# Loading the first x chunk and the first w1 tiles of an MLP in two pieces each, with fewer dummy matmuls before layer 1

## The chip, the cores and the metric

The kernel runs on one core of a Trainium2 chip. The metric is the device time of one execution in microseconds (us). Each call for runs also times the kernel before on the same chip. The profile of a run is of one execution; its span is about 1.3 us shorter than the time of that execution (93.4 against 94.75).

Each run carries a state. On one core a run is called slow when it is over 1.5% above the fastest run of the same kernel. That label comes from the time alone.

## The reference

```
B, S, D, F = 1, 2048, 448, 1792        # bf16
h   = gelu(x @ w1 + b1)                # layer 1: D = 3*128 + 64 in the contraction
out = h @ w2 + b2                      # layer 2
```

## The kernel before

All engines are programmed by hand with semaphores. x is worked on in four chunks of 512 rows. Chunks 1 to 3 are transposed by the DMA. The first chunk is loaded plainly into `xn`, turned on TensorE (12 transposes of 128x128, and two more for the 64 remainder columns), and copied from PSUM to `xT`. Until x is there, TensorE runs dummy matmuls on constants.

```python
NWARM = 7
W1CUTS = (0, 4, 8, 14)                        # w1's tiles of 128 columns per transfer

pr.dma("sync", lambda e: e.dma_start(xn[:, :, :], x0v), "x")      # whole first chunk, 448 KB
pr.barrier("sync", ["table"])                 # the rest waits for the activation table
load_w1r(0); load_w1(1); load_w1r(1); load_w1(2); ...             # SyncE's queue
load_w1(0, "scalar")                          # w1's first four tiles, 384 KB, ScalarE's queue
# ... cut ...
warm(NWARM)          # 7 dummies of 512 columns
warm(1, HC)          # one of 256
turn_all()           # 12 + 2 transposes, copies to xT on VectorE and ScalarE
warm(1, HC)          # one of 256
turn_b1()            # VectorE: bias to its layout
# VectorE: copy of half of w1's remainder rows to the other partitions, in two pieces
for i in (0, 1):
    ...  pr.op("vector", ... tensor_copy(odd(slice(0, H)), odd(slice(H, P))), after=[("w1r", i)], ...)
L = [Layer1(0, j) for j in range(NPAIR)]
for h in (0, HC):            # 24 matmuls of 256 columns, in pairs on 64 rows each (64*128 in the trace)
    L[0].a(h, h + HC)
    L[1].a(h, h + HC)
L[0].b()                     # 6 of 512 columns, then the pair on the remainder rows
L[2].a()
# ... cut: the rest of layer 1, layer 2, the other chunks: one unbroken stream of matmuls
```

Of the kernel before, what the change touches and what calls it, by code (L numbers as in the profile page):

```python
# [73 lines left out]
def bass_standalone__dense_activation_gelu__prompt_kernel(  # L74
# [8 lines left out]
    B, S, D = x.shape  # L83
# [4 lines left out]
    HC = SC // 2  # L88
# [4 lines left out]
    KT = 3  # L93
    D3 = KT * P
    DH = D // 2
    NWARM = 7

    with ExitStack() as es:
        sb = lambda name, shape, dt: es.enter_context(nc.sbuf_tensor(name, shape, dt))
        xn = sb("xn", [P, STC, D], BF16)  # L100
        xr = sb("xr", [P, STC // 2, P], BF16)
        ident = sb("ident", [P, P], BF16)
# [14 lines left out]
        pr = Program(nc, es)  # L117
# [2 lines left out]
        ones_m = one.broadcast_to([P, SC])  # L120


        W1CUTS = (0, 4, 8, 14)

        def w1_of(ft):
            return max(i for i, c in enumerate(W1CUTS) if c <= ft)

        def load_w1(i, engine="sync"):
            c0, c1 = W1CUTS[i] * P, W1CUTS[i + 1] * P
            pr.dma(engine, lambda e: e.dma_start(  # L130
                w1_sb[:, :, c0:c1], w1[0:D3, c0:c1].rearrange("(k p) f -> p k f", p=P)), ("w1", i))
# [3 lines left out]
        def load_w1r(i, engine="sync"):  # L135
            cs = slice(RCUTS[i] * P, RCUTS[i + 1] * P)
            pr.dma(engine, lambda e: e.dma_start(w1r[H:P, cs], w1[D3:D, cs]), ("w1r", i))

        def load_w2(a, b):
            pr.dma("sync", lambda e: e.dma_start(  # L140
                w2_sb[:, a:b, :], w2[a * P:b * P, :].rearrange("(f p) d -> p f d", p=P)), ("w2", a))
# [8 lines left out]

        x0v = x2[0:SC, :].rearrange("(p t) d -> p t d", t=STC)
        o0v = out2[0:SC, :].rearrange("(p t) d -> p t d", t=STC)
        pr.dma("sync", lambda e: e.dma_start(xn[:, :, :], x0v), "x")
        pr.barrier("sync", ["table"])
        load_w1r(0)
        load_w1(1)
        load_w1r(1)
        load_w1(2)
        load_w2(0, 7)
        load_w2(7, 14)  # L160
        pr.dma("sync", lambda e: e.dma_start(b2_bc[:, :], b2.partition_broadcast(P)), "b2")
        for c in range(1, NSC):
            for slot in range(KT + 1):
# [10 lines left out]
               after=["b1z"])  # L174
        pr.op("scalar", lambda e: e.activation(junk[:, :], one, ACT.Gelu_apprx_tanh), event="table")  # L175
        load_w1(0, "scalar")

        def turn_b1():
            for q in range(4):
                pr.op("vector", lambda e, q=q: e.transpose(  # L180
                    b1t[32 * q:32 * q + 32, :], b1n[:, 32 * q:32 * q + 32]), after=["b1n"], event=("b1t", q))
            pr.op("vector", lambda e: e.tensor_copy(b1_f[:, :], b1t[:, 0:NFT]),
                  after=[("b1t", q) for q in range(4)], event="b1")
# [5 lines left out]
        def warm(n, cols=SC):  # L189
            for _ in range(n):  # L190
                pr.op("tensor", lambda e: e.matmul(unit[0][:, 0, 0:cols], lhsT=ones_w, rhs=ones_m[:, 0:cols],  # L191
                                                   start=True, stop=True))
# [140 lines left out]
        def stage(t):  # L333
            return unit[3 - t // 2][:, t % 2, 0:2 * P].bitcast(BF16)

        def turn(t):
            for k in range(KT):
                pr.op("tensor", lambda e, k=k: e.transpose(  # L338
                    stage(t)[:, k * P:(k + 1) * P], xn[:, t, k * P:(k + 1) * P], ident[:, :]),
                    after=["ident", "x"], event=("xt", t) if k == KT - 1 else None)  # L340

        def evac(engine, t):
            o = xT[:, 0:KT, t * P:(t + 1) * P]
            i = stage(t)[:, 0:D3].rearrange("p (k s) -> p k s", k=KT)
            pr.op(engine, lambda e: e.copy(o, i) if engine == "scalar" else e.tensor_copy(o, i),  # L345
                  after=[("xt", t)], event=("xT0", t))
            busy[(3 - t // 2, t % 2)] = ("xT0", t)

        def turn_all():


            pr.op("vector", lambda e: e.tensor_copy(  # L352
                xr[:, :, :].rearrange("p q (two h) -> p q two h", two=2),
                xn[:, :, D3:D].rearrange("p (q two) h -> p q two h", two=2)), after=["x"], event="xr_in")
            for t in range(STC):
                turn(t)
                evac(("vector", "scalar")[t % 2], t)
            for q in range(STC // 2):
                pr.op("tensor", lambda e, q=q: e.transpose(  # L359
                    stage(0)[:, q * P:(q + 1) * P], xr[:, q, :], ident[:, :]),  # L360
                    after=["xr_in", ("xT0", 0)], event=("xr", q))
            halves = (slice(0, H), slice(H, P))
            for src, engine in enumerate(("vector", "scalar")):
                i = stage(0)[halves[src], 0:2 * P].rearrange("p (q s) -> p q s", q=2)
                for dst in (src, 1 - src):
                    o = xT[halves[dst], KT, 0:SC].rearrange("p (q two s) -> p q two s", q=2, two=2)[:, :, src, :]
                    pr.op(engine, lambda e, o=o, i=i, engine=engine:
                          e.copy(o, i) if engine == "scalar" else e.tensor_copy(o, i),  # L368
                          after=[("xr", 0), ("xr", 1)], event=("xR0", dst, src))
            busy[(3, 0)] = ("xR0", 1, 0)  # L370
            busy[(3, 2)] = ("xR0", 0, 1)

        warm(NWARM)
        warm(1, HC)
        turn_all()
        warm(1, HC)
        turn_b1()

        for i in (0, 1):
# [3 lines left out]
                  after=[("w1r", i)], event=("w1rU", i))  # L383
# [12 lines left out]
        for c in range(NSC):  # L396
# [7 lines left out]
            else:  # L404

                pr.op("vector", lambda e: e.tensor_copy(b2_z[H:H + 1, :], b2_bc[H:H + 1, :]),  # L406
                      after=["b2", "b2z0"], event="b2z")
# [3 lines left out]
            p = Layer2(c, (0, 1))  # L411
            if c + 1 < NSC:
                q = Layer2(c, (2, 3))
# [5 lines left out]
            else:  # L419
                q, r = Layer2(c, (2,)), Layer2(c, (3,), True)  # L420
# [37 lines left out]
```

## Time and profile before

Three runs gave 94.43 us (94.25 to 94.45), and the profiled execution took 94.75 us.

| what | value | where to read it |
|---|---|---|
| PE on the chain that ended last | 97% of 93.4 us | chain of waits |
| unbroken matmuls of the two layers | 5.86 to 91.27 us | chain of waits |
| x: issued, landed | 0.75, about 3.86 us | timeline and transfers (3.1 us to landing) |
| start of layer 1 | 5.79 us | timeline |
| layer 1's first 30 matmuls | 2.52 us | timeline |

The chain of work that ended last, in order of time; columns are start, length and what.

```profile
0.78 3.36 PE u L191 x8
4.14 1.29 PE u L338 x12
5.43 0.21 PE u L359 x2
5.65 0.21 PE u L191
5.86 85.41 PE u L216 x909
91.27 0.38 DVE out_sb L325
```

TensorE is the only engine on it until the last 0.38 us. The change can only act before 5.86 us. The timeline of PE at the start; columns are start, length, engine, line and operation, and `xN` counts merged instructions (L191 are dummies, L338 and L359 transposes, L216 the layers).

```profile
0.78 3.36 PE L191 MATMUL u<-const-bfloat16-1.0 128*128 128x512 bf16 x8 [0.78 <-PEq L443]
4.00 1.44 PE L338 MATMUL u<-ident,xn 128*128 128x128 bf16 x12
5.23 0.42 PE L359 MATMUL u<-ident,xr 128*128 128x128 bf16 x2
5.44 0.42 PE L191 MATMUL u<-const-bfloat16-1.0 128*128 128x256 bf16 x1
5.79 2.52 PE L216 MATMUL u<-xT,w_sb 64*128 64x256 bf16 x30
8.15 0.38 PE L216 MATMUL u<-xT,w1r 64*128 64x512 bf16 x2
```

The table of stretches shows why; the number behind PE's busy time counts the matmuls that touch the stretch, and the 1.00 before the DMA share is the granted clock.

```profile
5.80:6.60 0.80, 0.80 (x9) 0.58 (x10) 0.73 (x3) 0.75 (x3) 0.00 (x0) 1.00 0.89 255
6.60:7.40 0.80, 0.80 (x19) 0.69 (x14) 0.61 (x3) 0.14 (x1) 0.00 (x0) 1.00 0.88 234
```

Both stretches are fully busy with the same kind of matmul, yet the second holds twice as many. Single starts in the trace agree: pairs of 256 columns start 213 ns apart up to 6.6 us and 109 ns apart after. (The prediction's 208 and 107 count from the second start of a pair to the first of the next.) TensorE's rate doubled near 6.6 us. The column of the granted clock says 1.00 in both and does not show this: the packed trace of this execution holds no record of the clock (0 entries), and the view then prints 1.00.

### The profile page before, as it was taken

The numbers are of one execution on the slowest core, as the hardware profiler recorded it, in microseconds if no ns is written. First come the engines' busy times: TensorE is split into PE (matmuls) and PEld (weight loads), VectorE is DVE, ScalarE is ACT, GpSimd is POOL, SyncE is SP. The second block draws the span as 40 slices with busy tenths as digits, with TensorE's granted clock in tenths as the row PEclk, the third lists the DMA queues.
The fourth block names the chain that finished last, engine by engine and source line by source line (L and its number), as shares of the span: only waits on it lengthen the run. The fifth ranks groups of instructions, "written<-read, shape, count | busy, mean of one in ns | idle before, by whom it ended". The sixth has DMA issues, their size and how long they took to land.

```text
span 93.4 us, 2060 instructions
## 1 busy us (share of the span) xinstructions
PE 90.4 (97%) x932; PEld 46.5 (50%) x932; DVE 13.3 (14%) x33; ACT 38.5 (41%) x63; POOL 1.7 (2%) x8
## 2 busy tenths in 40 slices
PE   6999999999999999999999999999999999999990
PEld 2475444455544444454554444445544444475890
DVE  0173001010334000000234000000234000000421
ACT  6073787900002887900002888900001878910001
POOL 6000000000000000000000000000000000000000
DMA  2999999554748000000033000000022000000022
GB/s 51 358 275 292 360 309 151 113 113 91 83 86 217 7 0 0 7 0 0 0 102 101 0 0 4 0 7 0 0 98 98 0 0 7 0 0 7 18 80 98
DMA packets 12344, 7.32 MB, mean 78 GB/s; under 512 B 6960, under 2 KB 12144, under 8 KB 12336
## 3 DMA queue, kind: packets, MB, share of 16 engines
q1 hardware_dynamic: 11904, 6.80, 31.1%
q10 hardware_dynamic: 400, 0.39, 1.2%
q8 instruction: 7, 0.11, 0.5%
q14 instruction: 1, 0.01, 0.0%
q0 software_dynamic: 32, 0.00, 0.0%
HBM read 3.79 MB, written 1.84 MB: 60 GB/s over the span
## 4 chain that ended last, share of the span: by engine, by line
PE 97%; DVE 0%; issue 0%
PE u L216 91%; PE u L191 4%; PE u L338 1%; DVE out_sb L325 0%; PE u L359 0%
## 5 line engine op out<-in xcount | busy, mean ns | idle before, releaser
L268 ACT ACTIVATE g<-u,b_f 128x512 bf16<-128x512 f32 x56 | 35.0, 685 | 40.3 <-PE u L216 40.3
L216 PE MATMUL u<-w_sb,g 64*128 64x448 bf16 (+1 forms) x504 | 43.2, 328 | 0.0
L216 PE MATMUL u<-xT,w_sb 64*128 64x512 bf16 (+1 forms) x348 | 41.2, 372 | 0.0
L216 PEld LDWEIGHTS u<-w_sb,g 64*128 64x128 bf16 x504 | 24.4, 94 | 18.6
L216 PEld LDWEIGHTS u<-xT,w_sb 64*128 64x128 bf16 x348 | 16.9, 95 | 19.6 <-issue 0.3
L311 DVE TENSOR_TENSOR out_sb<-u,b_bc 128x448 bf16<-128x448 f32 x14 | 8.1, 619 | 60.6 <-PE u L216 60.6
L216 PE MATMUL u<-xT,w1r 64*128 64x512 bf16 x56 | 10.6, 376 | 0.0
L191 PE MATMUL u<-const-bfloat16-1.0 128*128 128x512 bf16 (+1 forms) x9 | 3.8, 578 | 0.8 <-PEq L443 0.8
L216 PEld LDWEIGHTS u<-xT,w1r 64*128 64x128 bf16 x56 | 2.7, 94 | 3.3
L328 ACT CAST out_sb<-u 128x224 bf16<-128x224 f32 x1 | 0.3, 346 | 9.2 <-PE u L216 9.2
L191 PEld LDWEIGHTS u<-const-bfloat16-1.0 128*128 128x128 bf16 x9 | 1.2, 138 | 2.4 <-issue 2.4
L345 ACT COPY xT<-u 128x384 bf16<-128x384 bf16 x2 | 1.0, 479 | 2.8 <-PE u L338 2.8
L175 ACT ACT_TABLE_LOAD x1 | 1.3, 1283 | 0.7 <-PEq L443 0.7
L338 PEld LDWEIGHTS u<-ident,xn 128*128 128x128 bf16 x12 | 1.2, 140 | 0.5 <-issue 0.5
L338 PE MATMUL u<-ident,xn 128*128 128x128 bf16 x12 | 1.4, 307 | 0.0
L186 DVE COPY xT<-xT 64x512 bf16<-64x512 bf16 x3 | 0.9, 290 | 3.5 <-DMA xT<-in_x_dram 3.5
L406 DVE COPY b_z<-b_bc 1x448 bf16<-1x448 bf16 x1 | 0.3, 267 | 6.8 <-DMA b_bc<-in_b_dram 6.8
L319 DVE TENSOR_TENSOR out_sb<-u,b_bc 128x448 bf16<-128x448 f32 x1 | 0.6, 625 | 1.7 <-PE u L216 1.7
L180 DVE STREAM_TRANSPOSE b1t<-b1n 32x32 bf16<-32x32 bf16 x4 | 0.8, 202 | 0.1
L345 DVE COPY xT<-u 128x384 bf16<-128x384 bf16 x2 | 0.7, 357 | 0.7 <-PE u L338 0.7
L368 ACT COPY xT<-u 64x256 bf16<-64x256 bf16 x2 | 0.7, 368 | 0.0
L352 DVE COPY xr<-xn 128x256 bf16<-128x256 bf16 x1 | 0.2, 227 | 3.0 <-DMA xn<-in_x_dram 3.0
(18 smaller groups left out, 5.0 us busy)
## 6 DMA issues: line engine op xcount, KB each, us to landing
out_dram<-out_sb SPq DMA_DIRECT2D x16, 112.0 KB, 1.7
w_sb<-in_w_dram SPq DMA_DIRECT2D x2, 784.0 KB, 8.7
w_sb<-in_w_dram SPq DMA_DIRECT2D x1, 576.0 KB, 6.4
xn<-in_x_dram SPq DMA_DIRECT2D x1, 448.0 KB, 3.1
w_sb<-in_w_dram ACTq DMA_DIRECT2D x1, 384.0 KB, 4.2
w_sb<-in_w_dram SPq DMA_DIRECT2D x1, 384.0 KB, 4.1
xT<-in_x_dram SPq DMA_TRANSPOSE x12, 4.5
w1r<-in_w_dram SPq DMA_DIRECT2D x1, 160.0 KB, 4.0
```

Of the source, the lines that this page charges most:

```text
L175: pr.op("scalar", lambda e: e.activation(junk[:, :], one, ACT.Gelu_apprx_tanh), event="table")
L180: pr.op("vector", lambda e, q=q: e.transpose(b1t[32 * q:32 * q + 32, :], b1n[:, 32 * q:32 * q + 32]), after=["b1n"], event=("b1t", q))
L186: pr.op("vector", lambda e: e.tensor_copy(xT[0:H, KT, s0:s1], xT[H:P, KT, s0:s1]), after=after, event=event)
L191: pr.op("tensor", lambda e: e.matmul(unit[0][:, 0, 0:cols], lhsT=ones_w, rhs=ones_m[:, 0:cols], start=True, stop=True))
L216: o = pr.op("tensor", lambda e: e.matmul(unit[u][:, lo, cols], lhsT=lhsT, rhs=rhs, start=start, stop=stop, skip_group_check=skip), after=a ...
L268: pr.op("scalar", lambda e, lo=lo, ft=ft: e.activation(g[:, ft, c * SC:(c + 1) * SC], unit[u][:, lo, :], ACT.Gelu_apprx_tanh, bias=b1_f[:, ...
L311: pr.op("vector", lambda e, lo=lo, j=j: e.tensor_tensor(out=out_sb[:, j, :], in0=unit[u][:, lo, 0:D], in1=b2_bc[:, :], op=ALU.add), after= ...
L319: pr.op("vector", lambda e: e.tensor_tensor(out=out_sb[:, j, :].rearrange("p (two h) -> p two h", two=2), in0=unit[u][:, :, 0:DH], in1=b2_ ...
L328: pr.op("scalar", lambda e: e.copy(out_sb[:, j, DH:D], unit[u][:, 1, 0:DH]), after=[y[1]], event=("o", j, 1))
L338: pr.op("tensor", lambda e, k=k: e.transpose(stage(t)[:, k * P:(k + 1) * P], xn[:, t, k * P:(k + 1) * P], ident[:, :]), after=["ident", "x ...
L345: pr.op(engine, lambda e: e.copy(o, i) if engine == "scalar" else e.tensor_copy(o, i), after=[("xt", t)], event=("xT0", t))
L368: e.copy(o, i) if engine == "scalar" else e.tensor_copy(o, i),
```

## The change

The intent is to start the transposes when the first half of x has landed, to let w1's first tiles arrive in smaller pieces, and to drop the dummies that an earlier x makes needless.

```diff
-    NWARM = 7
+    NWARM = 6
-        W1CUTS = (0, 4, 8, 14)
+        W1CUTS = (0, 2, 4, 8, 14)
-        pr.dma("sync", lambda e: e.dma_start(xn[:, :, :], x0v), "x")
+        for h in (0, 2):
+            pr.dma("sync", lambda e, h=h: e.dma_start(xn[:, h:h + 2, :], x0v[:, h:h + 2, :]), ("x", h))
         load_w1(0, "scalar")
+        load_w1(1, "scalar")
-                    after=["ident", "x"], ...)
+                    after=["ident", ("x", t // 2 * 2)], ...)
         warm(NWARM)
-        warm(1, HC)
         turn_all()
-        warm(1, HC)
         turn_b1()
# (cut: later w1 pieces renumbered; the remainder's copy on VectorE made per half of x)
```

More of the change, by code (lines that the diff above doesn't have):

```diff
@@ L152, in bass_standalone__dense_activation_gelu__prompt_kernel @@
         o0v = out2[0:SC, :].rearrange("(p t) d -> p t d", t=STC)
-        pr.dma("sync", lambda e: e.dma_start(xn[:, :, :], x0v), "x")
+        for h in (0, 2):
+            pr.dma("sync", lambda e, h=h: e.dma_start(xn[:, h:h + 2, :], x0v[:, h:h + 2, :]), ("x", h))
         pr.barrier("sync", ["table"])
         load_w1r(0)
-        load_w1(1)
+        load_w1(2)
         load_w1r(1)
-        load_w1(2)
+        load_w1(3)
         load_w2(0, 7)
@@ L339, in turn @@
                     stage(t)[:, k * P:(k + 1) * P], xn[:, t, k * P:(k + 1) * P], ident[:, :]),
-                    after=["ident", "x"], event=("xt", t) if k == KT - 1 else None)
+                    after=["ident", ("x", t // 2 * 2)], event=("xt", t) if k == KT - 1 else None)
         def evac(engine, t):
@@ L349, in turn_all @@
         def turn_all():
-            pr.op("vector", lambda e: e.tensor_copy(
-                xr[:, :, :].rearrange("p q (two h) -> p q two h", two=2),
-                xn[:, :, D3:D].rearrange("p (q two) h -> p q two h", two=2)), after=["x"], event="xr_in")
             for t in range(STC):
+                if t % 2 == 0:
+                    pr.op("vector", lambda e, t=t: e.tensor_copy(
+                        xr[:, t // 2, :].rearrange("p (two h) -> p two h", two=2), xn[:, t:t + 2, D3:D]),
+                        after=[("x", t)], event=("xr_in", t // 2))
                 turn(t)
@@ L360, in turn_all @@
                     stage(0)[:, q * P:(q + 1) * P], xr[:, q, :], ident[:, :]),
-                    after=["xr_in", ("xT0", 0)], event=("xr", q))
+                    after=[("xr_in", q), ("xT0", 0)], event=("xr", q))
             halves = (slice(0, H), slice(H, P))
```

## The prediction

> **What bounds it.** TensorE. The chain of waits puts 97% of the 93.4 us span on PE, 91% on the layer matmuls, in one unbroken piece from 5.86 to 91.27 us. The change touches only what comes before. In the timeline: dummies from 0.78 us, 12 transposes from 4.00, two for the remainder from 5.23, one dummy at 5.44, layer 1 from 5.79. The x transfer (issued 0.75) lands 3.1 us after its issue, about 3.86, so PE is fed by dummies just until x is there.
>
> **Clock.** The start-to-start times of single matmuls show two rates: dummies of 512 columns every 427 ns and transposes every 107 ns up to 5.44, and the first layer-1 pairs of 256 columns every 208 ns; from about 6.63 us the same pairs come every 107 ns. So about 0.84 us of layer 1 runs at half rate. [...]
>
> **What changes.** Removed from the PE queue: one full dummy (427 ns), the 256-column one before the transposes (213 ns) and the one after them (213 ns, plus about 0.14 us until layer 1 starts). Added: one transfer issue on each queue (0.39 and 0.45 us, off PE) and one small VectorE copy (the whole copy took 0.23 us). The bytes are the same; w1's pieces fall from 1024 to 512 bytes.
>
> **Order of transfers.** Before, w1's first packet came at 3.08 us, when x's were nearly done, although both were issued within 0.05 us. So I expect first half of x, first half of w1, second half of x, second half of w1; [...] Packets of x ran 1.77 to 3.37 us, those of w1 3.08 to 4.51, and landing is seen about 0.5 us after the last packet. My estimate: first half of x lands near 3.3, w1's first half 4.0, x's second half 4.5, w1's second half 5.2.
>
> **PE after.** Dummies end at 3.30, six transposes 3.35 to 4.0, PE idle about 0.5 us, six more 4.6 to 5.25, two remainder transposes to 5.46, layer 1 from about 5.6 instead of 5.79. So the second half of x, later than before, takes back most of the gain from the first. VectorE's chain (bias turn, remainder copy) still fits.
>
> **Worth.** 0.2 us earlier at the half rate is only 0.1 us if the rate still doubles near 6.6 us: about 94.3 us. The danger is the clock: [...] I give that one chance in three. If instead the halves of x land one behind the other (3.3 and 3.9), layer 1 starts near 5.0 and the gain is 0.4 us.
>
> **Prediction.** 94.3 us, range 93.6 to 96.1; faster by over 2%: 0.02, within 2%: 0.89, slower by over 2%: 0.09.
>
> **Right or wrong shows in:** the landing of the two halves of x (transfers view); an idle of PE of about 0.5 us between sixth and seventh transpose, put down to x; the start of layer 1 near 5.6; the moment when pairs of 256 columns fall from about 208 to 107 ns; an unchanged steady part from there to the end.
>
> **What would make it wrong:** [...] the second half of x landing before w1's first; 512-byte pieces so slow that w1's second half or the next w1 transfer stalls layer 1.

The sum came to 94.3 us: the 94.4 of before less 0.1 for a start 0.2 us earlier at the half rate. A term for a later doubling brought the sum to 96.0 us and was given one chance in three.

## The result, and the profile after

The changed kernel took 95.88 us (95.71 to 96.14, 4 runs) against 94.44 us; the ratio is 1.0152 (1.0118 to 1.0187). A ratio is the mean time of one kernel's fast runs over that of the other's in the same rounds, so it is not quite the ratio of the medians. By the 2% rule it counts as the same, but 1.4 us were lost.

The chain of waits after:

```profile
1.20 3.65 DMA xn<-in_x_dram
4.84 0.05 issue
4.89 0.82 PE u L340 x6
5.71 0.21 PE u L362 x2
5.93 86.30 PE u L218 x909
92.22 0.38 DVE out_sb L327
```

The second half of x is now on the chain and lands at 4.84 us. Still, the layers begin only 0.07 us later than before (5.93 against 5.86). The last matmul, however, is 0.95 us later (92.22 against 91.27). The timeline of PE, and the stretches:

```profile
0.78 2.72 PE L193 MATMUL u<-const-bfloat16-1.0 128*128 128x512 bf16 x6 [0.78 <-PEq L444]
3.68 0.80 PE L340 MATMUL u<-ident,xn 128*128 128x128 bf16 x6 [0.18 <-DMA xn<-in_x_dram]
4.89 0.82 PE L340 MATMUL u<-ident,xn 128*128 128x128 bf16 x6 [0.41 <-DMA xn<-in_x_dram]
5.50 0.42 PE L362 MATMUL u<-ident,xr 128*128 128x128 bf16 x2
5.86 3.42 PE L218 MATMUL u<-xT,w_sb 64*128 64x256 bf16 x30
9.11 0.38 PE L218 MATMUL u<-xT,w1r 64*128 64x512 bf16 x2
```

```profile
5.80:6.60 0.80, 0.80 (x10) 0.57 (x10) 0.53 (x2) 0.78 (x2) 0.00 (x0) 1.00 1.16 361
6.60:7.40 0.80, 0.80 (x12) 0.56 (x10) 0.68 (x5) 0.39 (x2) 0.00 (x0) 1.00 1.03 189
```

The 30 matmuls take 3.42 us instead of 2.52 and wait for nothing. In 6.60 to 7.40 there are 12 instead of 19: the rate is still low, and by the starts in the trace it doubles only near 8.5 us. So 0.90 us (3.42 less 2.52) and the 0.07 us of the later start make, to 0.01 us, the 0.96 us by which the spans differ (94.40 and 93.44). Nothing else in the kernel is slower: from the remainder pair on (8.15 and 9.11 us) to the last matmul both need the same time to 0.01 us. The other 0.5 us of the measured 1.44 has no trace: the profiled run was the slowest of the kernel before and the fastest of the changed one.

The ends of the two holes: by the semaphores in the trace the first half of x landed at 3.54, w1's first half at 4.15, x's second half at 4.84, w1's second half at 5.58 us. The single dummies stream for 427 ns each, so TensorE had nothing to do from 3.29 to 3.68 and from 4.27 to 4.89 us, 1.0 us together. (The profile's own idle of 0.18 and 0.41 is shorter because it lists a matmul for longer: the last dummy, started at 2.87, for 0.63 us.)

### The profile page after: what moved, and what is told of

Read it like the earlier page. It is cut to its first block, busy times and chain, and to the rows that moved or that the text cites. A ratio compares the mean times of both kernels' runs of the same rounds, so it can differ in the third digit from the quotient of the medians.

```text
span 94.4 us, 2057 instructions
## 1 busy us (share of the span) xinstructions
PE 90.8 (96%) x929; PEld 46.6 (49%) x929; DVE 13.6 (14%) x34; ACT 38.6 (41%) x63; POOL 1.7 (2%) x8
## 4 chain that ended last, share of the span: by engine, by line
PE 93%; DMA 4%; SPq 0%; DVE 0%; issue 0%
PE u L218 91%; DMA xn<-in_x_dram 4%; PE u L340 1%; SPq L154 0%; DVE out_sb L327 0%; PE u L362 0%
## 5 line engine op out<-in xcount | busy, mean ns | idle before, releaser
L218 PE MATMUL u<-xT,w_sb 64*128 64x512 bf16 (+1 forms) x348 | 42.1, 379 | 0.0
L218 PEld LDWEIGHTS u<-xT,w_sb 64*128 64x128 bf16 x348 | 17.4, 98 | 19.9 <-issue 0.2
L193 PE MATMUL u<-const-bfloat16-1.0 128*128 128x512 bf16 x6 | 2.7, 626 | 0.8 <-PEq L444 0.8
L193 PEld LDWEIGHTS u<-const-bfloat16-1.0 128*128 128x128 bf16 x6 | 0.7, 136 | 1.9 <-issue 1.9
```

The lines of the kernel that those rows point to most:

```text
L193: pr.op("tensor", lambda e: e.matmul(unit[0][:, 0, 0:cols], lhsT=ones_w, rhs=ones_m[:, 0:cols], start=True, stop=True))
L218: o = pr.op("tensor", lambda e: e.matmul(unit[u][:, lo, cols], lhsT=lhsT, rhs=rhs, start=start, stop=stop, skip_group_check=skip), after=a ...
```

## The experiments

Theories, by the names that the expectations use:

- A: idle of TensorE before layer 1 delays the doubling of its rate.
- B: the later half of x and the smaller pieces cost the time themselves.
- C: transposes do not count as activity; the amount of matmul work does.
- D: the moment of doubling falls by chance, alike in every kernel.
- E, formed on the way: both. Chance moves the moment of doubling from one execution to the next, and the kernel's holes let it come late in some or all of them.

The twelve runs were made in three calls, on three chips. The result above came from an earlier call; it is called the result's call.

### First call: holes filled, dummies alone, transfers alone

`fill_holes`: the changed kernel with its holes filled.

```diff
-    NWARM = 6
+    NWARM = 7
             for t in range(STC):
+                if t == 2:
+                    warm(2, HC)
                 turn(t)
```

> The changed kernel (transfers split, no dummy before layer 1) with dummies put into its two holes: a seventh full one at the start and two of 256 columns between the third and the fourth chunk-half (before the seventh transpose). Theory A (idle of TensorE before layer 1 delays the doubling of its clock): doubling back near 6.6 us instead of 8.6, layer 1 still from about 5.86, time 94.3 to 94.7 us. Theory B (the later second half of x and the smaller pieces cost the time themselves): 95.7 to 96.1, as the changed kernel. Theory C (transposes do not count as activity, only the amount of matmul work does): doubling earlier than in the changed kernel by about the 0.85 us of added dummies, 95.3 or so.

Measured: 94.65 us (94.48 to 94.76, 4 runs), before 94.21 (93.95 to 94.77, 7 runs), ratio 1.0032 (0.9987 to 1.0077). Layer 1 starts no earlier than in the changed kernel, and the transfers are the same, but the 30 matmuls take 2.13 us:

```profile
5.89 2.13 PE L218 MATMUL u<-xT,w_sb 64*128 64x256 bf16 x30
```

The changed kernel was not run in this call, so the two times alone can't be set against each other. The trace can: with the same transfers and as late a layer 1, its span is 93.4 us, as in the kernel before, so theory B is out as the explanation of the 1.4 us. The doubling came at 5.9 us, earlier than in the first trace of the kernel before, which A did not foresee.

`few_dummies`: the transfers of before, the dummies of the change.

```diff
-    NWARM = 7
+    NWARM = 6
         warm(NWARM)
-        warm(1, HC)
         turn_all()
-        warm(1, HC)
```

> The kernel before, transfers untouched, with only the dummies of the change: six full ones, none of 256 columns. One hole of about 0.65 us before the transposes, layer 1 from about 5.58 us. Theory A: the clock doubles later than 6.63 us (up to 8.6), time 95 to 96 us. Theory B: transfers are as before, so 94.3 us or a little less than before. Theory C: 1.07 us less... 0.85 us of dummies less, doubling 0.6 us or more later, about 94.7.

Measured: 94.36 us (93.88 to 94.52, 4 runs), ratio 0.9995 (0.9943 to 1.0047).

```profile
0.78 2.72 PE L191 MATMUL u<-const-bfloat16-1.0 128*128 128x512 bf16 x6 [0.78 <-PEq L441]
4.11 1.44 PE L338 MATMUL u<-ident,xn 128*128 128x128 bf16 x12 [0.60 <-DMA xn<-in_x_dram]
5.69 2.13 PE L216 MATMUL u<-xT,w_sb 64*128 64x256 bf16 x30
```

This is a miss for A in its simple form: 0.8 us without work (3.30 to 4.11), and the rate was still doubled when layer 1 began. It is also a miss for C: only six dummies came before, less matmul work than in any kernel above, and the doubling was early.

`split_only`: the transfers of the change, with all dummies of before (`NWARM = 7` and both of 256 columns).

> Only the transfers of the change: x and w1 in two pieces each, all dummies of the kernel before kept (seven, one of 256, one of 256 after the transposes). PE idle about 0.25 us before the seventh transpose, layer 1 from about 6.06 us. Theory A: doubling near 6.6 to 6.8 us, time 94.5 to 94.8 us. Theory B: 95.7 or more. Theory C: 94.5.

Measured: 94.56 us (94.28 to 94.71, 4 runs), ratio 1.0018 (0.9962 to 1.0074). The new transfers alone cost nothing that the runs resolve, though layer 1 starts at 5.88 us. They also gain nothing.

`long_dummies`: the kernel before with `NWARM = 20`, to watch the doubling under plain matmuls.

> The kernel before with 20 full dummies instead of 7, so that nothing but back-to-back matmuls runs for the first 6 us and more. Not meant to be fast: it shows when the clock doubles without transposes and without a hole. If [...] transposes count as activity: dummies go from 427 to 214 ns apart near 6.6 us, as in the kernel before. If transposes do not count (theory C): near 4 to 5 us.

Measured: 96.92 us (one run, state unknown; longer for the extra dummies). The dummies start 427 ns apart up to 4.15 us and about 219 apart from 4.52 on, so the rate doubled near 4.5 us. The transposes, now after the doubling, start 56 ns apart instead of 107. In the groups of the kernel before (L338, 311 ns) and of this one, the three numbers are the least, the median and the greatest duration in ns:

```profile
L338 PE MATMUL u<-ident,xn x12: 264/311/311, 4.0 to 5.1; 128*128 128x128 bf16 x12
```
```profile
L338 PE MATMUL u<-ident,xn x12: 217/219/220, 7.0 to 7.7; 128*128 128x128 bf16 x12
```

So transposes run at the doubled rate as other matmuls do. (They are the kernel's `transpose` calls; the trace lists them as MATMUL.) And in the same call the moment of doubling (4.5, and 5.6 to 5.9 in the three others) was not that of the first trace (6.6).

### Second call: the changed kernel again, one hole at a time, another order

`after_again`: the changed kernel, unchanged.

> The changed kernel once more, on the chip of this call, because the earlier experiments and the first result came from different calls and the moment of doubling moved between them (6.63 us in the first trace of the kernel before; about 5.6 us with few_dummies, split_only and fill_holes). Theory A [...]: 95.4 to 96.1 us here too, doubling after 7.5 us. Theory D (the moment of doubling falls by chance, whatever the kernel, and the changed kernel had bad luck in its first call): like few_dummies, 94.3 us, doubling near 5.6 us.

Measured: 94.43, 94.35, 94.40, 94.29, 95.89 and 94.51 us; before 94.55 (94.08 to 94.83, 11 runs). The ratio of 0.9983 (0.9956 to 1.001) hides that there are two groups. The profiled run was an early one:

```profile
3.85 0.67 PE L340 MATMUL u<-ident,xn 128*128 128x128 bf16 x6 [0.35 <-DMA xn<-in_x_dram]
5.04 0.51 PE L340 MATMUL u<-ident,xn 128*128 128x128 bf16 x6 [0.52 <-DMA xn<-in_x_dram]
5.59 2.13 PE L218 MATMUL u<-xT,w_sb 64*128 64x256 bf16 x30
7.57 0.74 PE L218 MATMUL u<-xT,w1r 64*128 64x512 bf16 x2
```

It is the same program as in the first profile after, with the same two holes, and its rate doubled at 4.3 us, among the transposes (a gap of 74 ns after gaps of 107), instead of 8.5. So the kernel alone does not fix the moment. Theory A alone is out. The last line shows a second thing: the remainder pair now waits about 0.14 us, because the copy on VectorE that it needs was timed for a later layer 1 (the next start comes after 359 ns instead of 216). This takes back part of the gain of an early doubling.

`fill_first` (the changed kernel with `NWARM = 7`) and `fill_second` (the changed kernel with the two dummies before the seventh transpose, `NWARM = 6`):

> The changed kernel with seven dummies instead of six: its first hole of 0.39 us closed, the second (now 0.5 us) left. Theory A: the total idle before layer 1 falls from 1.0 to 0.55 us, less than in few_dummies (0.8), which doubled early: so 94.4 to 94.8 us. Theory D: the same as after_again.

> The changed kernel with two dummies of 256 columns before the seventh transpose: its second hole of 0.62 us nearly closed (0.2 left), the first of 0.39 us left. Theory A, by the sum of idle alone: 94.4 to 94.8 us, as fill_first. If it is one hole's place that matters, the two runs differ by about 1 us. Theory D: the same as after_again.

Measured: 94.52 us (94.34 to 94.70, 6 runs) and 94.42 us (94.34 to 94.66, 6 runs), ratios 0.9995 (0.9969 to 1.0021) and 0.9987 (0.9959 to 1.0015). In their traces the doubling came near 6.3 and 6.0 us:

```profile
5.89 2.29 PE L218 MATMUL u<-xT,w_sb 64*128 64x256 bf16 x30
5.83 2.21 PE L218 MATMUL u<-xT,w_sb 64*128 64x256 bf16 x30
```

None of the twelve runs was late. That does not yet show that one hole alone is harmless: in this call only one of six runs of the changed kernel, with both holes, was late, and none of twelve is no surprise beside that.

`x_first`: to bring x's second half ahead of w1, everything on SyncE's queue.

```diff
+        load_w1(0)
+        load_w1(1)
         pr.barrier("sync", ["table"])
-        load_w1(0, "scalar")
-        load_w1(1, "scalar")
-    NWARM = 6
+    NWARM = 7
```

> A version that may beat both: the two halves of x and then the two pieces of w1, all on SyncE's queue, seven dummies. x's second half should land near 4.0 us instead of 4.84, since no piece of w1 goes before it, w1's second piece near 5.5 as in the changed kernel; no hole before the transposes; layer 1 from about 5.25 us. If the clock has doubled by then, 93.9 us; if it doubles near 6.6, 94.2. A stall of 0.2 to 0.4 us at the remainder step of the first pair of tiles is likely (the copy on VectorE is late).

Measured: 94.85 us (94.69 to 95.35, 6 runs), ratio 1.0037 (1.0007 to 1.0067). The two halves of x landed at 3.39 and 3.91 us, as hoped, and the rate doubled at 4.7 us in the middle of the transposes. But w1's pieces landed at 5.45 and 6.08 us and its next transfer at 8.90, and layer 1 had to wait for them:

```profile
5.49 2.43 PE L218 MATMUL u<-xT,w_sb 64*128 64x256 bf16 x30 [0.37 <-DMA w_sb<-in_w_dram]
8.95 0.60 PE L218 MATMUL u<-xT,w_sb 64*128 64x512 bf16 x4 [0.81 <-DMA w_sb<-in_w_dram]
```

Putting these pieces on one queue only moved the wait from x to w1.

### Third call: the two groups, a hole alone, two attempts at a better kernel

`after_third`: the changed kernel once more.

> The changed kernel a third time. So far 4 of 4 timed runs near 95.9 us in the first call and 1 of 6 in the second; the other five near 94.4. Theory E [...]: two groups again, near 94.4 and near 95.9 us and little between, in a share that chance decides. Theory D (chance alone, every kernel alike): then the kernel before should show runs near 95.9 too, which it has not in 22 runs.

Measured: 95.94, 96.03, 94.31, 95.64, 96.00 and 95.83 us, with a granted clock of 1.0 in the profiled one; before 94.01 (93.81 to 94.81, 11 runs). Because one run is at 94.31, the four above 95.7 are labelled slow here. The ratio of 1.008 (0.9998 to 1.0163) is of one run from each group and means nothing. The profiled run, of the late group, doubled near 8.65 us:

```profile
6.11 3.36 PE L218 MATMUL u<-xT,w_sb 64*128 64x256 bf16 x30
```

The size of the holes does not part the two groups: by the starts they add up to 1.01 us in the first trace after and 1.26 us here, both late, and to 1.24 us in `after_again`, which was early.

Over the result's call and the two here the changed kernel had 10 of 16 runs at 95.64 to 96.14 us and 6 at 94.29 to 94.51, none between. The kernel before had 33 runs over all four calls, none above 94.83; in the three calls that had both kernels it was 26 runs, none late, against 10 of 16. Kernels with the changed transfers and at least one hole filled (`fill_holes`, `fill_first`, `fill_second`, `split_only`) had 20 runs, none above 94.76, but 8 of them in a call without the changed kernel and 12 in the call where it was late once. Theory D is out.

`four_dummies`: the kernel before with a hole and nothing else.

```diff
-    NWARM = 7
+    NWARM = 4
         warm(NWARM)
-        warm(1, HC)
         turn_all()
-        warm(1, HC)
```

> The kernel before, transfers untouched, with four full dummies and no other: TensorE works from 0.78 to 2.44 us, then sits idle about 1.6 us until x is there (few_dummies, with six, sat idle 0.8 us and was as fast as the kernel before). Theory E: [...] 94.9 to 96.5 us, none near 94. Theory B (transfers) and D (chance): as few_dummies, 93.9 to 94.5 us.

Measured: 95.77, 95.20, 94.92, 95.44, 96.11 and 95.35 us, ratio 1.0132 (1.0086 to 1.0178). Layer 1 starts earlier than before, at 5.58 us, and the 30 matmuls take 3.76 us:

```profile
0.79 1.86 PE L191 MATMUL u<-const-bfloat16-1.0 128*128 128x512 bf16 x4 [0.79 <-PEq L441]
4.00 1.44 PE L338 MATMUL u<-ident,xn 128*128 128x128 bf16 x12 [1.35 <-DMA xn<-in_x_dram]
5.58 3.76 PE L216 MATMUL u<-xT,w_sb 64*128 64x256 bf16 x30
```

No transfer was touched. Taking dummies away, which only makes idle, is enough to lose 1.3%. Theory E said every run late, between 94.9 and 96.5 us, none near 94; that is what came (94.92 to 96.11), while the kernel before had 11 runs in this call, none above 94.81.

`copy_early`: the kernel before, with VectorE's first remainder copy ahead of the turning of b1.

```diff
-        turn_b1()
         for i in (0, 1):
+            if i:
+                turn_b1()
             odd = ...
```

> The kernel before with one VectorE step moved: the copy of w1's remainder rows that layer 1 needs first goes ahead of the turning of b1. Where the clock doubles early, layer 1 was seen to stall 0.14 us for it (few_dummies; 355 against 216 ns between two pairs). Expected gain up to 0.15 us in runs that double early, nothing in the others: ratio 0.998 to 1.000.

Measured: 94.24 us (93.96 to 94.83, 6 runs), ratio 1.0012 (0.9968 to 1.0057). Inconclusive: no gain is seen. Its trace doubled near 6.7 us, where the copy is in time anyhow.

`x_then_w1`: x in halves, w1's four tiles in one transfer on ScalarE's queue, held back until the activation table is loaded.

```diff
-        load_w1(0, "scalar")
+        load_w1(0, "scalar", ["table"])
# and x in two halves, NWARM = 7, no dummies of 256 columns, the copy early
```

> A version that may beat both: x in two halves on SyncE's queue; w1's first four tiles in one transfer on ScalarE's queue, but issued only after the activation table (about 2.2 us), so that it doesn't get between the halves of x; seven dummies, no hole; copy of the remainder rows early as in copy_early. First half of x should land near 3.5, second near 4.0, w1 near 5.0 to 5.2; layer 1 from about 5.35 us instead of 5.69 to 5.79. 93.9 to 94.2 us, no run near 95.9. If w1 comes later than 5.4, no gain.

Measured: 95.05, 95.18, 95.22, 96.94, 96.61 and 95.59 us, ratio of the fast runs 1.011 (1.0065 to 1.0156). The two highest are labelled slow, 96.94 with a granted clock of 0.982; what made them so is not known. A miss. x landed at 3.39 and 3.91 us and the transposes were done early, but w1, issued at 2.27 us in the company of SyncE's next transfers, landed at 6.45 instead of about 5, and TensorE waited:

```profile
6.49 2.13 PE L217 MATMUL u<-xT,w_sb 64*128 64x256 bf16 x30 [1.07 <-DMA w_sb<-in_w_dram]
```

No version beat the kernel before.

### All traces against theory E

Eight of the 14 packed traces hold a record of the clock. It begins with a stretch at full clock, and where the starts of matmuls resolve the doubling, this stretch begins within about 0.02 us of it.

For each trace I take the moment of doubling from this record (marked *) or, where there is none, read it from the starts, which draw together. (In `x_then_w1` TensorE was idle at that moment; only the record shows it.) Beside it stand the start and length of layer 1's first 30 matmuls, from the timeline of PE.

| kernel | rate doubles near, us | the 30 matmuls start, us | they take, us |
|---|---|---|---|
| changed, second call | 4.25* | 5.59 | 2.13 |
| long_dummies | 4.46* | 8.23 | 2.13 |
| x_first | 4.7 | 5.49 | 2.43, with waits for w1 |
| few_dummies | 5.64* | 5.69 | 2.13 |
| split_only | 5.64* | 5.88 | 2.13 |
| fill_holes | 5.90* | 5.89 | 2.13 |
| fill_second | 6.03* | 5.83 | 2.21 |
| x_then_w1 | 6.07* | 6.49 | 2.13 |
| fill_first | 6.3 | 5.89 | 2.29 |
| before | 6.6 | 5.79 | 2.52 |
| copy_early | 6.7 | 5.89 | 2.50 |
| changed, result's call | 8.55 | 5.86 | 3.42 |
| changed, third call | 8.65 | 6.11 | 3.36 |
| four_dummies | 8.94* | 5.58 | 3.76 |

No trace lies between 6.7 and 8.55 us. The three late ones are of the two kernels with 1.0 us or more of idle before the last transpose: 1.01 and 1.26 us in the changed kernel, about 1.6 in `four_dummies` (from 2.44 us, when its dummies have streamed, to the first transpose at 4.00). But the changed kernel with 1.24 us also gave the earliest doubling of all. `few_dummies`, with 0.8 us, doubled at 5.64, and none of its 4 runs was late. That is what E says in outline: chance moves the moment, and enough idle lets it come late. How much idle is enough, over what time it counts, and what chance acts on, the traces do not show.

## Why the prediction was right or wrong

The 95.88 us lie in the range of 93.6 to 96.1, and the clock, through which the loss came, was named as the danger. The central figure of 94.3 was not met. The range holds both groups of runs, so it would have held the result whichever came; that the late one came was a draw, as the second call shows (five of six runs at 94.29 to 94.51 us).

- The order of transfers was right: x, w1, x, w1. The times were put too early: 3.3, 4.0, 4.5 and 5.2 us expected, 3.54, 4.15, 4.84 and 5.58 measured.
- Hence the hole of "about 0.5 us" was two holes of 0.39 and 0.62 us. The start of layer 1 "from about 5.6" was 5.86 us, so there was no gain at the start but a loss of 0.07 us.
- "Only 0.1 us if the rate still doubles near 6.6 us" failed in its condition. The prediction took 6.6 us, read from one trace, for a property of the kernel. It was one draw: kernels without holes doubled between 4.5 and 6.7 us in other traces.
- "The danger is the clock": this is what the late group shows (doubling at 8.55 and 8.65 us; 95.64 to 96.14 us). "One chance in three" looks low beside 10 runs of 16, but the share went from one in six to four in four between calls.
- "An unchanged steady part" was right: it differs by 0.01 us.

Settled by the runs: the loss is the late doubling of TensorE's rate, not a wait for the transfers; idle made by fewer dummies alone brings it about (`four_dummies`: 8.94 us, 94.92 to 96.11 us a run); in the changed kernel it comes in some executions and not in others. That the changed kernel's own holes are the cause there rests on `four_dummies` as a parallel and on 20 runs with a hole filled, none late, of which none was made in a call where the changed kernel was mostly late; `fill_first` and `fill_second` in such a call would settle it. Still open is what sets the moment in an execution: why four of four executions were late in the result's call, one of six in the second and five of six in the third. Nothing in the runs tells a chip from an hour from plain luck. Also open is how much idle it takes.

## What to carry to other kernels

Dummy matmuls at the start do not only fill time: without enough of them the rate of TensorE can double late. Here four dummies instead of nine put the doubling at 8.94 us instead of 6.6 (one trace each), and one full microsecond of holes or more in the first six was followed by a late run in 10 of 16 executions, while 0.8 us (`few_dummies`) was not in any of 4. Before thinning them out for an earlier first load, sum the holes that the new landings leave, and judge the change by many runs on several calls, looking for two groups, since four runs here said 1.5% slower and six later ones said no difference. The earlier first half of a transfer was worth nothing here (3.54 us, but 4.84 for the second half, against 3.86 for the whole): the next step needed both, and it began 0.07 us later.
